# Fourier mixing and an ELU layer on one core: VectorE's combinations and transposes at other places of the order, one small transfer on GpSimd's queue

## The chip, the cores and the metric

The kernel runs on one core of a Trainium2 chip. The core has TensorE (matrix products; the profile calls its matmuls PE and its weight loads PEld), VectorE (DVE), ScalarE (ACT), GpSimd (POOL) and a queue engine, SyncE (SP), which here only issues transfers. The metric is the device time of one execution in microseconds (us): the median over eight runs. Lower is better.

## The reference

```python
def _attn_ref(x):                       # x: (8, 3008, 256) float32
    X = np.fft.fft(x, axis=1)
    X = np.fft.fft(X, axis=2)
    return X.real.astype(np.float32)

def _moe_ref(x, w_in, w_out):           # x: (24064, 256)
    h = x @ w_in                        # w_in (256, 2048)
    g = np.where(h > 0.0, h, np.exp(np.minimum(h, 0.0)) - 1.0)
    return (g @ w_out).astype(np.float32)   # w_out (2048, 256)
```

The result of the first goes, as 24064 rows of 256, into the second. The two weight matrices arrive as 64-bit floats.

## The kernel before

**Work.** The transform along the sequence is done as products with cosine and sine matrices (`Dft`); the one along the channels is folded into `w_in`, which becomes a cosine part `Wc` and a sine part `Ws`. Symmetry lets one column serve two output rows: h is P plus Q for one row and P minus Q for its mirror, with P from `Wc` and Q from `Ws`. Transformed columns are kept in three rings, `Rr` (real part), `Ir` (imaginary part, the "sine ring") and `Rb` (channel 128 on all partitions). Channel 128 has no row in the 128-row product; its weights are the last row of `Ws`, which is carried to columns of `wex` through a scratch row in memory, `wx` (`spread_last_row`, line 389: two transfers per chunk of 256 columns, the second of which waits for the first).

**Steps and tiles.** A tile is 256 columns; there are 47. Each takes eight steps, each for 256 of the 2048 hidden units, so 376 steps in all. A step is spread over three periods of the order: `mm_P` (TensorE, bank `H`), `even_part` (two VectorE instructions that add channel 128's part, `E <- Rb, wex, H`, line 714), `mm_Q` (adds Q to the same bank, and therefore must follow `even_part`), `h_minus` (VectorE, line 724), exponentials on ScalarE, `g_plus` and `g_minus` (VectorE, line 740), four sums on GpSimd (`sum_1`, `sum_3`, `sum_2`, `sum_4`, line 362), and the second product with `w_out`. This one is done in Winograd's way, with seven products instead of eight: `mm_X1` writes banks `pA` and `pB`, `mm_X2` writes `pC` and `pD`, and they gather over the eight steps of a tile. At a tile's end VectorE combines the banks: `comb_1` makes `u` from `pA` (through a copy by ScalarE) and `pB`; `comb_2` makes `v` from `u` and `pC`; `comb_22` adds `v` and `pC` into half of `u`; `comb_3` adds `pD` to `v`. Then `turn_u` and `turn_v` transpose `u` and `v`, and SP stores them. The first tile has the plain eight products, and the first eight steps also run beside the preparation of the weights.

**Order.** Everything runs in an order written out by hand: `at(t, fn)` puts a function at time t, in units of about one microsecond, and the list is sorted and emitted once. A period `T` is 4.8 units. Each engine works through its own instructions in this order, so t decides only who stands before whom on an engine. Within a step's first period VectorE has `even_part` at 0.9, then of the step before `g_plus` at 2.2 and `g_minus` at 2.9, then `h_minus` at 3.55. TensorE has `mm_P` at 0, `mm_X1` of two steps before at 0.87, `mm_Q` at 2.17, `mm_X2` at 3.04, and at 4.75 in some steps half of a `Dft`, whose results VectorE puts into the rings at 1.01 and 1.02 of the next period (`plus`, `minus`).

**Weights.** A weight chunk passes through `fields` (VectorE), `power` (ScalarE), `round` and `scale` (VectorE or GpSimd) (lines 203 to 270). Folded input sums are made by `fold_x`; `EO1` and `EO3` are the sums that the odd frequencies need.

Of the kernel before, what the change touches and what calls it, by code (L numbers as in the profile page):

```python
# [77 lines left out]
def kernel(  # L78
# [7 lines left out]
    nc = tc.nc  # L86
# [78 lines left out]
    Ws = cpool.tile([128, NDFF], FP, tag="Ws")  # L165
# [177 lines left out]
    wx_dr = dpool.tile([1, NDFF], FP, tag="wx", name="wx")  # L343
# [44 lines left out]

    def spread_last_row(q):
        c = slice(q * 256, (q + 1) * 256)  # L390
        nc.sync.dma_start(out=wx_dr[:, c], in_=Ws[127:128, c])
        with nc.allow_non_contiguous_dma(reason="one row to columns"):
            nc.sync.dma_start(
                out=wex[:, 2 * q : 2 * q + 2],
                in_=wx_dr[:, c].rearrange("o (f p) -> p (o f)", p=128),
            )
# [608 lines left out]
    def fold_now(keys):  # L1005
        for key in keys.split():
            ops[key, 0]()
# [9 lines left out]
    def at(t, fn):  # L1017
        events.append((t, len(events), fn))

    def at_chunk(t, chunk):  # L1020
        at(t, chunk.fields)
        at(t + 0.01, chunk.power)
        at(t + 0.02, chunk.round)
        at(t + 1.4, chunk.scale)
# [31 lines left out]
        dft_now(state["x_even"], 0, "pD")  # L1056

    at(-12.8, begin_x_even)
    at(-12.6, lambda: spread_last_row(0))
    at(-11.0, lambda: fold_now("O2 o0 o1 O0 EO2"))  # L1060
    at_chunk(-10.0, w1_chunks[1])
    at(-8.5, R_even.copy)
# [6 lines left out]
    at(-5.8, lambda: state["x_even"].minus())  # L1069
    at(-5.7, lambda: nc.sync.dma_start(out=Ir[127:128, 0:RUN], in_=Rb[127:128, 0:RUN]))  # L1070
    at_chunk(-5.0, w1_chunks[2])
    at(-1.9, lambda: fold_now("EO1 EO3"))
    at(-1.7, w1_chunks[6].load)
    at(-1.6, w1_chunks[7].load)
    at(-1.5, w2_chunks[3].load)
# [3 lines left out]
    T = PERIOD  # L1079
    for chunk, k, second in (  # L1080
        (w1_chunks[3], 0, 0),
        (w2_chunks[0], 0, 1),
        (w1_chunks[4], 1, 0),
        (w2_chunks[1], 1, 1),
        (w1_chunks[5], 2, 0),
        (w2_chunks[2], 2, 1),
        (w1_chunks[6], 3, 0),
        (w2_chunks[3], 3, 1),
        (w1_chunks[7], 4, 0),
        (w2_chunks[4], 4, 1),  # L1090
        (w2_chunks[5], 5, 1),
        (w2_chunks[6], 6, 1),
        (w2_chunks[7], 7, 1),
    ):
        t = k * T + (1.0 if second else -0.5)
        at(t, chunk.fields)
        at(t + 0.02, chunk.power)
        at(t + 0.05, chunk.round)
        at(k * T + (3.7 if second else 1.7), chunk.scale)
    for c in range(1, 8):  # L1100
        t = (c - 2) * T + 4.7 if c > 1 else 1.0
        at(t, lambda c=c: fold_chunk(c))
        t = (c - 1) * T + 1.4 if c > 1 else 2.0
        at(t, lambda c=c: put_chunk(c))
        at(t + 0.01, lambda c=c: spread_last_row(c))
# [13 lines left out]
    for i in range(total):  # L1119
        t = i * T  # L1120
# [20 lines left out]
    COMB = (  # L1141
        (1.45, comb_copy),
        (4.2, comb_1),
        (T + 1.0, comb_2),
        (T + 1.1, comb_22),
        (T + 1.2, comb_3),
    )
    for q in range(n_tiles):
        t = (8 * q + 9) * T
        for dt, fn in (COMB if q else ((1.45, plain_u), (T + 1.1, plain_v))) + (  # L1150
            (2 * T + 1.0, turn_u),
            (3 * T + 1.0, turn_v),
        ):
            at(t + dt, lambda fn=fn, q=q: fn(q))

# [55 lines left out]
    for n in range(16):  # L1211
        j, k = divmod(n, 4)
# [87 lines left out]
```

## Time and profile before

| | |
|---|---|
| median of 8 runs | 2009.41 us (2008.33 to 2011.47) |
| profiled execution | 2007.74 us, of it 2006.0 us span |
| TensorE matmuls busy | 1975.1 us, 98% of the span |
| VectorE busy | 1277.3 us, 64% |
| ScalarE busy | 860.8 us, 43% |
| GpSimd busy | 1330.3 us, 66% |
| share of the chain that ended last | TensorE 92%, transfers 3%, VectorE 2%, GpSimd 1%, ScalarE 1% |
| transfers | 71.6 MB, mean 36 GB/s; the 16 transfer engines are near full in the first 36 us |

The span runs from the first to the last instruction of one profiled execution. Busy times overlap. An engine's idle time is put down to what ended it. Matmul records overlap too, so a busy TensorE can still lose time between two matmuls: the distance from one start to the next has to be read. A 128x256 product in this kernel is two matmul instructions, and their starts stand 0.216 us apart when nothing holds them.

### The profile page before, as it was taken

How to read it: one execution, taken by the hardware profiler on the slowest of the kernel's cores; microseconds unless marked ns; L12 is line 12 of the kernel's file. 1: busy time of each engine (PE TensorE's matmuls, PEld its weight loads, DVE VectorE, ACT ScalarE, POOL GpSimd, SP SyncE). 2: the span in 40 equal slices, each digit the busy share in tenths (PEclk: the TensorE clock that was granted, in tenths of full speed). 3: DMA queues.
4: the chain of work that ended last, by engine and by line, in shares of the span. 5: the costliest groups of instructions: out<-in, count | busy, mean ns of one | idle time of the engine just before them, and what ended most of it. 6: DMA issues, size and time to landing. Idle time of an engine off the chain costs nothing.

```text
span 2006.0 us, 26767 instructions
## 1 busy us (share of the span) xinstructions
PE 1975.1 (98%) x8895; PEld 1655.3 (83%) x8896; DVE 1277.3 (64%) x2342; ACT 860.8 (43%) x1651; POOL 1330.3 (66%) x1818
## 2 busy tenths in 40 slices
PE   8899999999999999999999999999999999999997
PEld 4788888888888888888888888888888888888886
DVE  7866656666566656666566665666556665666665
ACT  2544444443444444444444443444434444444443
POOL 2577757776577766777567775678657776555564
PEclk9999999999999999999999999999999999999999
DMA  8227200121001110011100211003010110000101
GB/s 318 85 20 64 48 16 13 38 60 22 13 19 43 45 29 11 18 47 43 26 18 13 65 24 26 11 19 90 7 19 11 23 18 15 15 11 16 18 11 21
DMA packets 256253, 71.60 MB, mean 36 GB/s; under 512 B 244512, under 2 KB 245302, under 8 KB 255604
## 3 DMA queue, kind: packets, MB, share of 16 engines
q1 hardware_dynamic: 253780, 57.32, 14.5%
q0 software_dynamic: 2336, 12.59, 1.9%
q8 instruction: 70, 1.15, 0.2%
q14 instruction: 67, 0.55, 0.1%
HBM read 45.02 MB, written 24.80 MB: 35 GB/s over the span
## 4 chain that ended last, share of the span: by engine, by line
PE 92%; DMA 3%; DVE 2%; POOL 1%; ACT 1%; issue 1%; DVEq 0%; SPq 0%; POOLq 0%; ACTq 0%
PE H L353 37%; PE pB L353 16%; PE pC L353 16%; PE pD L353 15%; PE pA L353 8%; DMA wx<-Ws 1%; POOL G L362 1%; DVE E L714 1%; DMA xl<-in_x_dram,ix 1%; DMA wex<-wx 0%; DMA w<-in_moe_w_out_dram 0%; DVE G L740 0%; DMA xl<-in_x_dram 0%; POOL xl L144 0%; ACT w L365 0%
## 5 line engine op out<-in xcount | busy, mean ns | idle before, releaser
L362 POOL TENSOR_TENSOR G<-G 128x256 f32<-128x256 f32 x1472 | 1055.4, 728 | 599.9 <-DVE G L740 438.0
L714 DVE SCALAR_TENSOR_TENSOR E<-Rb,wex,H 128x256 f32<-128x256 f32 x752 | 328.0, 478 | 647.2 <-PE H L353 642.7
L365 ACT ACTIVATE G<-H 128x512 f32<-128x512 f32 x376 | 224.5, 597 | 969.4 <-DVE G L724 969.4
L353 PE MATMUL H<-Ir,Ws 128*128 128x256 f32 x1504 | 387.7, 380 | 13.7 <-DVE E L714 13.7
L353 PE MATMUL H<-Rr,Wc 128*128 128x256 f32 x1504 | 386.4, 379 | 0.0
L353 PE MATMUL pC<-G,WT 128*128 128x256 f32 x1472 | 381.1, 381 | 2.3 <-DVE u L359 2.3
L353 PEld LDWEIGHTS H<-Ir,Ws 128*128 128x128 f32 x1504 | 278.8, 190 | 62.2 <-DVE E L714 16.8
L353 PEld LDWEIGHTS H<-Rr,Wc 128*128 128x128 f32 x1504 | 285.1, 190 | 53.2 <-issue 2.5
L353 PEld LDWEIGHTS pC<-G,WT 128*128 128x128 f32 x1472 | 276.0, 190 | 52.8 <-issue 13.6
L740 DVE SCALAR_TENSOR_TENSOR G<-G,H 128x512 f32<-128x512 f32 x376 | 253.4, 674 | 33.4 <-ACT G L365 32.2
L724 DVE SCALAR_TENSOR_TENSOR G<-E,H 128x512 f32<-128x512 f32 x376 | 256.0, 681 | 25.4 <-PE H L353 0.9
L740 DVE SCALAR_TENSOR_TENSOR G<-M,G 128x512 f32<-128x512 f32 x376 | 256.4, 682 | 0.0
L353 PE MATMUL pA<-G,w 128*128 128x256 f32 x800 | 234.2, 379 | 0.5 <-issue 0.5
L353 PE MATMUL pB<-G,w 128*128 128x256 f32 x800 | 234.0, 379 | 0.0
L365 ACT ACTIVATE G<-G 128x512 f32<-128x512 f32 x376 | 233.3, 620 | 0.0
L353 PE MATMUL pB<-G,WT 128*128 128x256 f32 x736 | 224.3, 386 | 1.4 <-POOL G L362 1.3
L365 ACT ACTIVATE M<-G 128x512 f32<-128x512 f32 x376 | 224.3, 596 | 0.0
L365 ACT ACTIVATE M<-M 128x512 f32<-128x512 f32 x376 | 221.0, 588 | 0.1
L353 PE MATMUL pD<-G,w 128*128 128x256 f32 x736 | 218.9, 379 | 0.0
L353 PE MATMUL pD<-G,WT 128*128 128x256 f32 x736 | 218.9, 379 | 0.0
L353 PEld LDWEIGHTS pA<-G,w 128*128 128x128 f32 x800 | 151.8, 190 | 21.9 <-POOL w L362 0.9
L353 PEld LDWEIGHTS pB<-G,w 128*128 128x128 f32 x800 | 152.0, 190 | 20.7
(134 smaller groups left out, 1329.2 us busy)
## 6 DMA issues: line engine op xcount, KB each, us to landing
out_dram<-ot SPq DMA_DIRECT2D x504, 32.0 KB
xl<-in_x_dram SPq DMA_DIRECT2D x16, 768.0 KB
MC<-dft_mats SPq DMA_DIRECT2D x4, 1131.0 KB
out_dram<-ot SPq DMA_DIRECT2D x256, 2.0 KB
Rb<-r SPq DMA_DIRECT2D x10, 376.0 KB
raw<-in_moe_w_in_dram SPq DMA_DIRECT2D x6, 512.0 KB
raw<-in_moe_w_out_dram SPq DMA_DIRECT2D x6, 512.0 KB
out_dram<-ot SPq DMA_DIRECT2D x64, 28.0 KB
```

Source lines behind the costliest of these rows:

```text
L353: nc.tensor.matmul(out_, lhsT=lhsT, rhs=rhs, start=start, stop=stop, skip_group_check=True)
L362: pin(nc.gpsimd.tensor_tensor(out=o, in0=a, in1=b, op=op))
L365: pin(nc.scalar.activation(out=o, in_=i, func=func, **kw))
L714: nc.vector.scalar_tensor_tensor(out=S.E[:, c], in0=Rb[:, cols(i)], scalar=wex[:, f : f + 1], in1=S.H[:, c], op0=ALU.mult, op1=ALU.add,)
L724: nc.vector.scalar_tensor_tensor(out=two(S.G[:, 0:512])[:, :, ::-1], in0=two(S.E), scalar=2.0, in1=two(S.H), op0=ALU.mult, op1=ALU.subtract,)
L740: nc.vector.scalar_tensor_tensor(out=o, in0=e, scalar=-1.0, in1=h, op0=ALU.add, op1=ALU.max)
```

## The change

Five things move; no arithmetic is added or taken away.

1. The first chunk's last row (`spread_last_row(0)`) is issued by GpSimd's queue instead of SP's, and earlier in the order (from -12.6 to -13.05, just behind `put_chunk(0)`, which writes that row).
2. The odd sums `EO1`, `EO3` go from -1.9 to 0.5, behind the first write of the sine ring (`I_even.plus`, `minus`, at 0.0 and 0.1).
3. `fields`, `power` and `round` of the weight chunk of step 0 (`w1_chunks[3]`) go from -0.5 to 0.3, also behind those writes.
4. At a tile's end `comb_2` and `comb_22` go from behind the next step's `even_part` to ahead of it, directly behind `comb_1`; `comb_3` goes from ahead of `g_plus` to behind it.
5. `turn_u` and `turn_v` go from behind `even_part` to behind `h_minus` of the same period.

```diff
     def spread_last_row(q):
         c = slice(q * 256, (q + 1) * 256)
-        nc.sync.dma_start(out=wx_dr[:, c], in_=Ws[127:128, c])
+        queue = nc.sync if q else nc.gpsimd
+        queue.dma_start(out=wx_dr[:, c], in_=Ws[127:128, c])
         with nc.allow_non_contiguous_dma(reason="one row to columns"):
-            nc.sync.dma_start(
+            queue.dma_start(
                 out=wex[:, 2 * q : 2 * q + 2],
...
-    at(-12.6, lambda: spread_last_row(0))
+    at(-13.05, lambda: spread_last_row(0))
...
-    at(-1.9, lambda: fold_now("EO1 EO3"))
+    at(0.5, lambda: fold_now("EO1 EO3"))
...
-        t = k * T + (1.0 if second else -0.5)
+        t = k * T + (1.0 if second else 0.3 if k == 0 else -0.5)
...
     COMB = (
         (1.45, comb_copy),
         (4.2, comb_1),
-        (T + 1.0, comb_2),
-        (T + 1.1, comb_22),
-        (T + 1.2, comb_3),
+        (4.21, comb_2),
+        (4.22, comb_22),
+        (T + 2.5, comb_3),
     )
...
-            (2 * T + 1.0, turn_u),
-            (3 * T + 1.0, turn_v),
+            (2 * T + 4.2, turn_u),
+            (3 * T + 4.2, turn_v),
```

## The prediction

> **What bounds the kernel.** I read the page's shares first (matmuls busy 98% of the span, TensorE 92% of the chain), so time can come only from places where TensorE loses starts. The view of waits names them (who waited for what: us in total, times, longest):
>
> ```profile
> DVE E L714 <- PE H L353: 642.7, 367, 3.9
> ...
> PEld pB L353 <- POOL G L362: 17.6, 52, 1.0
> ...
> PE H L353 <- DVE E L714: 13.7, 7, 7.0
> ...
> PEld pC L353 <- issue: 13.6, 42, 0.3
> ...
> DVE E L714 <- DMA wex<-wx: 4.5, 3, 2.9
> ```
>
> VectorE waits for `mm_P` nearly every step, 1.75 us each: the gap ahead of `even_part` that the change wants to fill. TensorE waits at three places: once 7.0 us at the start, 42 times for `pC`, 52 times for `pB`. I then read the timeline of VectorE and TensorE at one tile's end (start, length, what; idle before it in brackets):
>
> ```profile
> 361.91 0.68 DVE L724 SCALAR_TENSOR_TENSOR G<-E,H 128x512 f32<-128x512 f32 x1
> ...
> 362.50 0.68 DVE L359 TENSOR_TENSOR u<-p,pB 128x512 f32<-128x512 f32 x1
> ...
> 364.09 0.87 DVE L714 SCALAR_TENSOR_TENSOR E<-Rb,wex,H 128x256 f32<-128x256 f32 x2 [0.91 <-PE H L353]
> ...
> 364.88 0.68 DVE L359 TENSOR_TENSOR v<-u,pC 128x512 f32<-128x512 f32 x1
> 365.01 0.79 PEld L353 LDWEIGHTS H<-Ir,Ws 128*128 128x128 f32 x4
> 365.18 1.03 PE L353 MATMUL H<-Ir,Ws 128*128 128x256 f32 x4
> 365.59 0.42 DVE L359 TENSOR_TENSOR u<-v,pC 128x256 f32<-128x256 f32 x1
> 366.05 0.69 DVE L359 TENSOR_TENSOR v<-v,pD 128x512 f32<-128x512 f32 x1
> 366.13 0.73 PEld L353 LDWEIGHTS pC<-G,WT 128*128 128x128 f32 x4 [0.32 <-issue]
> 366.16 1.10 PE L353 MATMUL pC<-G,WT 128*128 128x256 f32 x4
> ...
> 369.75 0.30 PEld L353 LDWEIGHTS pB<-G,WT 128*128 128x128 f32 x2 [0.30 <-POOL G L362]
> ```
>
> Four matmuls take 0.86 us from start to start, but 0.98 from `mm_Q` (365.18) to `pC` (366.16), and 0.94 on to `pD`: 0.19 lost. The profile says "issue"; the row that ends just before, at 366.01, is `comb_22`, the last reader of `pC`. A step later the weight load for `pB` waits for GpSimd's `sum_2`, late because `g_plus` and `g_minus` stood behind three combinations: 0.17 lost. A weight load that starts x late costs x - 0.12 (0.31 late cost 0.19; 0.28 late cost 0.17).
>
> **Combinations, what goes.** The timelines of all 45 ends at which another step follows show the `pC` loss: 45 x 0.19 = 8.6 us; in three of them (near 980, 1027, 1432 us) ring writes stand between `comb_2` and `comb_22` and it is some 0.85 more each: 2.5. The `pB` loss follows 37 ends: 37 x 0.17 = 6.1. Together 17.2.
>
> **What is added: the combinations ahead of `even_part`.** `mm_Q`'s weight load in ordinary steps starts 0.05-0.06 after `even_part` ends, so it has only 0.07 to spare. From `comb_1`'s start to `even_part` there are 1.59 us (362.50 to 364.09). `comb_2` depends on `comb_1`, `comb_22` on `comb_2`: 0.71 each, as 364.88 to 365.59 shows. `comb_22` to `even_part` is independent; independent rows stand 0.08 closer than their length (0.68 long, 0.59 or 0.60 apart), so 0.34. Sum 1.76: `even_part` 0.17 to 0.18 late, TensorE loses 0.11. The distance is 1.56 to 1.59 at 28 ends: 3.1 us. At 9 ends VectorE is already late from ring writes and the distance is 1.10 to 1.25 (mean 1.20): 0.56 late, 0.49 lost, 4.4 us. At 8 ends half a `Dft` stands ahead of `mm_P` and it is 3.5 to 3.8: nothing. Sum 7.5. The bounds of this unseen adjacency: nothing if the load could go on the first half of `even_part`; 0.12 more per end (37 x 0.12 = 4.4) if `comb_22` is followed as by `comb_3`, 0.46 later. I take 0.34, the spacing of independent rows.
>
> `pC` is ready: its last matmul of the tile ends near 362.3. **`comb_3`** behind `g_plus` starts at 362.50 + 1.76 + 0.79 + 0.60 = 365.65 and ends at 366.34; `pD`'s load is due at 366.8. Behind it `g_minus` ends at 366.93 instead of 367.93; two sums of 0.75 after it end near 368.5, and `pB` needs them at 369.5, so that loss goes. At the three ends with ring writes `comb_3` ends near 980.96 where the load is due at 980.5: 0.45 each, 1.4 in all. Net of the combinations: 17.2 - 7.5 - 1.4 = 8.3 us.
>
> **Transposes**: 94 x 0.70 us, hidden in the gap of 1.85 us (1.2 after ring writes). If that cover were gone each would cost up to 0.6. Beside GpSimd's work one already takes 0.70 (374.73, under an L425 row). Their 1272 stores leave SP some 2.4 us later; SP issues 16 in 9.5 us, twice per 38 us. Last tile: same sequence. Nothing.
>
> **The start.**
>
> ```profile
> 23.39 0.30 SPq L391 DMA_DIRECT2D wx<-Ws  x1
> ...
> 30.53 1.57 POOL L362 TENSOR_TENSOR w<-raw,w 128x512 f32<-128x512 f32 x1 [26.21 <-ACT w L365]
> 30.87 2.04 DVE L425 TENSOR_TENSOR o<-o,o 128x762 f32<-128x762 f32 x1
> ...
> 38.51 0.87 DVE L714 SCALAR_TENSOR_TENSOR E<-Rb,wex,H 128x256 f32<-128x256 f32 x2 [2.94 <-DMA wex<-wx]
> ...
> 39.44 2.08 PE L353 MATMUL H<-Ir,Ws 128*128 128x256 f32 x4 [7.04 <-DVE E L714]
> ```
>
> The row is written at 18.8, goes out at 23.39 and lands at 35.45 (12.06 us in the chain); the second transfer takes 2.9 more. Only then runs the first `even_part`, and TensorE stands 7.04 us. Here a rule speaks against the change. The row: SP's queue holds whole matrices ahead of these 1 KB, and earlier GpSimd's two loads of x, 1.5 MB, landed in 10.55 us beside 3.3 MB of SP's. The Trainium skill (DMA: Bandwidth & Descriptors, "Issuing engines are not separate DMA queues") says that transfers from all engines share the same 16 engines and that a second issuer saves little but issue time. By it `wex` still lands near 38 and nothing is gained; by the row a second queue gets its turns between the first one's packets. I take the row. Issue 19.1, two transfers: the low end is GpSimd's shortest landing, 1.9 us each (near 23); the high end is 16 packets of 4 bytes per engine in turn with packets of 0.35 us (the longest kind in the transfer records here), 16 x 0.36 + 2 for the second and 4 for the first (near 31). Either is before 35.5, GpSimd's own next work is at 30.53, and SP's loads behind the removed pair go out 6 us sooner, for steps 15 us away or more.
>
> Then VectorE's own order binds. Ring writes wait for ScalarE's copy (30.83): 30.87 to 31.86. Chunk fields 0.75, `EO1`/`EO3` 1.9. The 2.04 row (its like takes 0.95) and GpSimd's 1.57 (1.29 alone) show that such pairs hold each other up; one GpSimd product of 1.1 falls between. Sum: 31.86 + 0.75 + 1.1 + 1.9 = 35.6, against 38.51: 2.9 us. TensorE's chain from there to 48.46 is back to back and later waits hang on it, so the shift stays.
>
> The clock (busy us per engine, then granted clock, transfer share, GB/s):
>
> ```profile
> 32.00:36.00 4.00, 0.39 (x2) 0.00 (x0) 3.56 (x5) 1.65 (x3) 1.96 (x2) 0.96 0.99 403
> 36.00:40.00 4.00, 0.56 (x1) 0.50 (x2) 1.49 (x5) 0.39 (x2) 1.29 (x1) 0.50 0.76 259
> 40.00:44.00 4.00, 4.00 (x11) 2.63 (x10) 3.10 (x6) 2.68 (x6) 2.37 (x2) 0.69 0.65 227
> ```
>
> After the idle stretch the clock is half until 42.5, so 3.05 us of work cost 1.5 more. The Trainium skill (TensorE: Matmul & The Clock Gate, "What's actually happening") has one idle window of 3.4 us, free-running, lower the clock. By the trace's row alone any idle of this kind costs 1.5; by the rule the 4.1 us that remain (32.4 to 36.5) hold a whole window only in (4.1 - 3.4) / 3.4 = a fifth of phases. I take the rule: 1.5 gained; if the clock still falls, -1.5 to +1.5. The start: 4.4 us.
>
> **Sum.** 8.3 + 4.4 = 12.7 us. The profiled execution, 2007.7 us (span 2006.0), would become 1995.0; its time is 1.7 below the median, so the median goes from 2009.4 to **1996.7**.
>
> **Rivals.**
> - `wex` through GpSimd lands no sooner than 38.5, or the half clock eats it: the start gives nothing, 2001.1. For: the shared engines, full until 38 us. Against: GpSimd's loads above. With the dearer 0.46 spacing too, 2005.5. Chance 0.23.
> - `even_part`'s lateness is free: 1996.7 - 7.5 = 1989.2. For: it has two halves. Against: the load stands 0.05 behind the second one's end in every ordinary step. Chance 0.09.
> - Slower: `comb_2` is released only when the next `mm_P` is through, so `even_part` is 1.05 late at 37 ends: 37 x 0.98 - 7.5 = 28.8 more, 2025.5. It decides from about 0.66 us lost per end. Against: in the last tile `comb_2` starts at 1993.48, 0.03 after `pC`'s matmul ends. Chance 0.08.
> - The forecast: 0.60, own range 1993 to 2000.
>
> What a measurement tells from no change is about 0.2%, 4 us: 2005.4 to 2013.4. The first rival reaches into that band with its dear end (0.10 in all). Range 1989 to 2005.5.
>
> **What would show it.** `PEld pC <- issue` and most of the 52 `pB` waits gone; a new `PEld H <- DVE E` wait of about 0.2 at some 28 ends and 0.55 at 9; `even_part` first at 35.6; granted clock 1 from 36 to 42. If the `H` waits exceed 0.6 on average, or the first `E` still waits for `wex`, the forecast is wrong there.

## The result, and the profile after

The changed kernel takes 1998.92 us (median of 11 runs, 1997.54 to 2006.24) against 2010.1 us (32 runs). By these medians it is 11.2 us less; the forecast was 12.7 us less, 1996.7 us. The ratio that is given here and below weighs all runs and is not that of the medians; three of the 11 runs lie above 2005 us. It is 0.9952, 95% interval 0.9943 to 0.9961: 9.6 us less, between 7.8 and 11.5. The profiled execution took 1999.07 us, 1997.3 of it span.

The waits of the whole changed kernel (who waited for what: us in total, times, longest):

```profile
PEld H L353 <- DVE E L715: 29.2, 44, 5.2
...
PE H L353 <- DVE E L715: 9.0, 14, 2.4
...
PE H L353 <- DMA Ir<-Rb: 4.8, 1, 4.8
...
DVE E L715 <- DMA wex<-wx: 1.9, 2, 1.4
...
PEld pB L353 <- POOL G L362: 1.7, 3, 0.9
PEld pD L353 <- PE pC L353: 1.7, 3, 0.6
```

The 42 waits at `pC` are gone and of 52 at `pB` 3 are left. In their place 44 weight loads of `mm_Q` wait for `even_part`, and three of `pD` wait at ends with ring writes. In the kernel before, the first of these lines read:

```profile
PEld H L353 <- DVE E L714: 16.8, 8, 7.4
```

At the start a transfer that no wait of before named, `Ir<-Rb`, now ends TensorE's longest wait, of 4.8 us. It brings the row of channel 128 from `Rb` into the sine ring, which `mm_Q` reads. The two waits for `wex` that are left belong to later chunks; the first `even_part` no longer waits for it.

The timeline of the changed kernel at the tile's end that the prediction read:

```profile
361.87 0.68 DVE L359 TENSOR_TENSOR u<-p,pB 128x512 f32<-128x512 f32 x1
...
362.65 0.69 DVE L359 TENSOR_TENSOR v<-u,pC 128x512 f32<-128x512 f32 x1
...
363.37 0.42 DVE L359 TENSOR_TENSOR u<-v,pC 128x256 f32<-128x256 f32 x1
...
363.71 0.86 DVE L715 SCALAR_TENSOR_TENSOR E<-Rb,wex,H 128x256 f32<-128x256 f32 x2
...
364.50 0.68 DVE L741 SCALAR_TENSOR_TENSOR G<-G,H 128x512 f32<-128x512 f32 x1
364.63 0.73 PEld L353 LDWEIGHTS H<-Ir,Ws 128*128 128x128 f32 x4 [0.32 <-DVE E L715]
364.63 1.13 PE L353 MATMUL H<-Ir,Ws 128*128 128x256 f32 x4
365.09 0.68 DVE L359 TENSOR_TENSOR v<-v,pD 128x512 f32<-128x512 f32 x1
```

The chain is 0.78 + 0.72 + 0.34 = 1.84 us long, where the prediction had 0.71 + 0.71 + 0.34 = 1.76. `even_part` no longer waits for anything: it is late. It ends at 364.57, the weight load of `mm_Q` starts 0.06 us later, and TensorE's starts lose 0.19 us here.

To part the start from the rest I use `comb_1`, which runs once per tile from the second on. The view of tile `u`, first of the kernel before, then of the changed one (count, shortest/median/longest in ns, first and last start in us):

```profile
L359 DVE TENSOR_TENSOR u<-p,pB x46: 677/679/686, 152.5 to 1992.7; 128x512 f32<-128x512 f32 x46
```

```profile
L359 DVE TENSOR_TENSOR u<-p,pB x46: 677/679/687, 152.7 to 1983.9; 128x512 f32<-128x512 f32 x46
```

From the first to the last it is 1840.2 us before and 1831.2 after, 9.0 less. The first comes no sooner, 152.7 against 152.5. In this execution the tiles' ends bring all and the start nothing.

The start of the changed kernel, in its timeline:

```profile
28.41 0.62 SPq L1071 DMA_DIRECT2D Ir<-Rb  x1
...
36.49 0.86 DVE L715 SCALAR_TENSOR_TENSOR E<-Rb,wex,H 128x256 f32<-128x256 f32 x2
...
37.52 2.04 PE L353 MATMUL H<-Ir,Ws 128*128 128x256 f32 x4 [4.81 <-DMA Ir<-Rb]
...
39.36 3.95 PE L353 MATMUL pA<-MC,e 128*128 128x376 f32 x6
```

`even_part` is 2.0 us sooner (38.51 before), `mm_Q` 1.9 (39.44). `even_part` ended at 37.35, so the transfer itself held `mm_Q` for little more than 0.1 us; both come at nearly the same time. But the six matmuls of `pA` now take 3.95 us (2.65 before). The windows of the changed kernel show why (busy us of PE, PEld, DVE, ACT, POOL, then granted clock, transfer share, GB/s):

```profile
32.00:36.00 4.00, 0.72 (x4) 0.29 (x2) 4.00 (x4) 1.92 (x3) 2.70 (x2) 1.00 0.99 402
36.00:40.00 4.00, 2.48 (x6) 1.86 (x7) 3.01 (x7) 2.28 (x5) 0.40 (x1) 0.54 1.04 386
40.00:44.00 4.00, 4.00 (x9) 2.27 (x8) 3.96 (x5) 2.32 (x5) 3.99 (x3) 0.61 0.61 196
```

The clock is half from 36.3 to 43.2 us. Work now falls into 5.6 us of that, not 3.05, and loses 2.8 us, not 1.5. So of 1.9 us, 0.6 are left at the second step's `even_part` (47.83 against 48.48). The changed kernel has one more stretch of half clock, 77.3 to 80.7 us, which this profile of the kernel before has not. The fifth step's `mm_Q`, just before it is through, still comes 0.5 us sooner (77.42 against 77.96); the sixth's comes at the same time (86.03 against 86.01) and waits for nothing but TensorE's own work. So the rest was lost in between, where that stretch lies.

### The profile page after: what moved, and what is told of

It reads as the page before. It is cut to its first block, busy times and chain, and to the rows that moved or that the text cites. A ratio compares the mean times of both kernels' runs of the same rounds, so it can differ in the third digit from the quotient of the medians.

```text
span 1997.3 us, 26765 instructions
## 1 busy us (share of the span) xinstructions
PE 1968.9 (99%) x8895; PEld 1662.0 (83%) x8896; DVE 1284.7 (64%) x2342; ACT 861.3 (43%) x1651; POOL 1336.5 (67%) x1820
## 3 DMA queue, kind: packets, MB, share of 16 engines
q8 instruction: 70, 1.15, 0.2%
## 4 chain that ended last, share of the span: by engine, by line
PE 93%; DVE 4%; ACT 1%; DMA 1%; issue 1%; POOL 0%; DVEq 0%; ACTq 0%; POOLq 0%; SPq 0%
PE H L353 38%; PE pB L353 16%; PE pD L353 16%; PE pC L353 15%; PE pA L353 8%; DVE E L715 1%; PE M L353 1%; DVE G L741 1%; DVE u L359 0%; DMA Ir<-Rb 0%; DVE v L359 0%; DVE G L725 0%; ACT G L365 0%; DMA wx<-Ws 0%; DVE w L220 0%
## 5 line engine op out<-in xcount | busy, mean ns | idle before, releaser
L353 PE MATMUL H<-Ir,Ws 128*128 128x256 f32 x1504 | 392.4, 383 | 13.8 <-DVE E L715 9.0
L353 PE MATMUL pB<-G,WT 128*128 128x256 f32 x736 | 219.2, 379 | 0.5 <-POOL G L362 0.5
L353 PEld LDWEIGHTS pB<-G,w 128*128 128x128 f32 x800 | 152.7, 191 | 21.0
```

The costliest lines, as they stand in the source:

```text
L353: nc.tensor.matmul(out_, lhsT=lhsT, rhs=rhs, start=start, stop=stop, skip_group_check=True)
```

## The experiments

Theory A, formed from the two traces: the gain is all at the tiles' ends, and at the start the sine ring's row and the half clock leave nothing of it. Theory B, the recorded forecast: the start carries 3 to 4 us. All ratios are to the kernel before, run on the same chip.

**Tiles' ends alone, start alone.** `steady_only` is the kernel before with the `COMB` and `turn` lines of the change's diff, `start_only` with the others.

> Parts 4 and 5 of the change alone (combinations, transposes), the start as before. Theory A (all of the gain is at the tiles' ends; the start's two us are lost again to the sine ring's row and the half clock): 8 to 9.5 us faster than before, the same time as the changed kernel within 1.5 us. Theory B (the start carries some 3 to 4 us of it): 5 to 6 us faster than before, 3 to 4 us slower than the changed kernel. In the trace under both: TensorE loses no start at pC, some 0.19 us at 27 ends and 0.56 at 9 ahead of mm_Q.

> Parts 1 to 3 alone (row on GpSimd's queue, odd sums and chunk fields behind the sine ring), tiles' ends as before. Theory A: 0 to 1.5 us faster than before; first even_part near 36.5 us, mm_Q near 37.5, waiting for the transfer Ir<-Rb. Theory B: 3 to 4 us faster.

Measured: `steady_only` 0.9959 (0.9947 to 0.9972), 8.2 us faster; `start_only` 0.9997 (0.9988 to 1.0005), not told from no change. The view of tile `u` of `steady_only` and of `start_only`:

```profile
L359 DVE TENSOR_TENSOR u<-p,pB x46: 678/681/689, 152.9 to 1985.7; 128x512 f32<-128x512 f32 x46
```

```profile
L359 DVE TENSOR_TENSOR u<-p,pB x46: 680/681/689, 153.0 to 1993.5; 128x512 f32<-128x512 f32 x46
```

1832.8 us between first and last, as in the changed kernel within 1.6, and 1840.5, as before. Of the 1.6, 1.2 are one wait for channel 128 in this execution of `steady_only`. Theory A holds and theory B is refuted: by the 95% interval of `start_only` the start is worth 2.4 us at most. Whether it is worth anything stays open; the medians differ by 1.5 us (2008.67 against 2010.15). In `start_only` the first `even_part` ran at 36.62 us, and `mm_Q` at 37.94, 0.4 behind its end. The profile puts this wait down to a VectorE instruction that `mm_Q` does not read (`pow`, line 214), not to `Ir<-Rb` as was expected.

**comb_22 behind even_part.**

```diff
         (4.21, comb_2),
-        (4.22, comb_22),
+        (T + 1.0, comb_22),
         (T + 2.5, comb_3),
```

> The changed kernel with comb_22 alone put back behind even_part (T + 1.0); comb_2 stays ahead of it. Theory A (TensorE loses what even_part comes late by: chain 0.78 + 0.72 + 0.34 = 1.84 us against 1.58 there): the chain becomes 0.78 + 0.60 = 1.4 us, so the 27 losses of 0.19 go and the 9 of 0.56 become some 0.15; pC's load is due 0.5 us after comb_22's end, so no wait returns: 8 to 10 us faster than the changed kernel, near 1989.5. Rival: comb_22 was not what made it late, or pC's wait comes back: within 2 us of the changed kernel.

Measured: 0.9911 (0.9898 to 0.9923), median 1991.1 us; 0.0041 below the changed kernel's ratio, 8.2 us. Its timeline at the same end:

```profile
360.04 0.68 DVE L359 TENSOR_TENSOR u<-p,pB 128x512 f32<-128x512 f32 x1
...
360.82 0.69 DVE L359 TENSOR_TENSOR v<-u,pC 128x512 f32<-128x512 f32 x1
...
361.62 0.87 DVE L715 SCALAR_TENSOR_TENSOR E<-Rb,wex,H 128x256 f32<-128x256 f32 x2
...
362.41 0.41 DVE L359 TENSOR_TENSOR u<-v,pC 128x256 f32<-128x256 f32 x1
362.55 0.79 PEld L353 LDWEIGHTS H<-Ir,Ws 128*128 128x128 f32 x4
...
363.36 0.62 PEld L353 LDWEIGHTS pC<-G,WT 128*128 128x128 f32 x3
```

`even_part` starts 1.58 us behind `comb_1`, as it did in the kernel before; `mm_Q`'s load has no wait, and `comb_22` ends at 362.82, half a microsecond before `pC`'s load. Its waits:

```profile
PEld H L353 <- DVE E L715: 17.3, 17, 4.9
...
PEld pD L353 <- PE pC L353: 2.7, 3, 0.9
```

17 loads wait for `even_part`, not 44. By the starts of TensorE's matmuls the losses ahead of `mm_Q` fell from 10.5 us to about 1. Those at `pD`, at the three ends with ring writes, grew from 1.3 to 2.3, where `comb_22` now runs between `even_part` and `comb_3`. That `even_part`'s lateness is the change's main price is thereby shown, and all but 1 us of it could have been avoided. From the first to the last `comb_1` it takes 1822.9 us, 8.3 less than in the changed kernel.

**TensorE kept busy at the start.**

```diff
+    def keep_busy():
+        t = bank("pB")
+        for _ in range(18):
+            mm(t, zero, zero[:, 0:1].to_broadcast([128, 512]), True)
+
+    at(2.1, keep_busy)
```

> The changed kernel with 18 matmuls of zeros added ahead of the first mm_Q, in TensorE's idle stretch (their result is not used). Theory A (the clock falls to half after the idle stretch and stays there to about 43 us, costing up to 2.8 us): granted clock 1 from 32 to 44 us, pA's first six matmuls 1.9 us instead of 3.7, 1 to 3 us faster than the changed kernel and less spread. Rival (the half clock costs nothing since the later steps wait for VectorE, ScalarE and transfers anyway): same time within 1 us though the clock is whole.

Measured: 0.9944 (0.9932 to 0.9957), median 1997.01 us; the interval overlaps the changed kernel's, so by time alone it is not told from it. The trace tells more; its windows and its view of `u`:

```profile
32.00:36.00 4.00, 4.00 (x20) 2.02 (x19) 4.00 (x5) 1.92 (x3) 2.84 (x3) 1.00 0.99 404
36.00:40.00 4.00, 3.12 (x13) 1.90 (x11) 4.00 (x9) 2.10 (x5) 0.21 (x1) 1.00 1.03 384
40.00:44.00 4.00, 4.00 (x16) 2.81 (x16) 3.13 (x4) 2.32 (x5) 4.00 (x3) 1.00 0.64 220
```

```profile
L359 DVE TENSOR_TENSOR u<-p,pB x46: 680/681/687, 150.2 to 1981.5; 128x512 f32<-128x512 f32 x46
```

`mm_Q` starts no sooner (37.59) and the clock stays whole. The second step's `mm_Q`, first in the changed kernel, then here:

```profile
48.76 1.13 PE L353 MATMUL H<-Ir,Ws 128*128 128x256 f32 x4 [0.97 <-DVE E L715]
```

```profile
46.06 1.13 PE L353 MATMUL H<-Ir,Ws 128*128 128x256 f32 x4 [0.96 <-DVE E L715]
```

From the first `mm_Q` to the second it is 8.5 us, not 11.2: the 2.8 that half of 5.6 us says. The first `comb_1` comes 2.5 us sooner than in the changed kernel. In the nine profiled executions without these matmuls (the kernel before among them) it came between 151.7 and 154.4 us. So the trace shows the gain, but the times do not, and the spread of the runs, which was expected to shrink, did not (1996.36 to 2004.52).

**Combinations alone, transposes alone.** The two parts of `steady_only`.

> The kernel before with the combinations moved as in the change (part 4) and nothing else; the transposes stay behind even_part. Theory A (the waits at pC and pB both come from the three combinations; the transposes are hidden at either place): as fast as steady_only within 1.5 us, 8 to 9 us faster than before, hardly any wait of pB at the tiles' ends. Rival (the transposes are what makes g_minus and the sum for pB late): the waits of pB stay, 2 to 3 us faster than before only.

> The kernel before with the transposes alone moved (part 5). Theory A: within 1 us of before; waits at pC and pB as before. Rival: some 6 us faster, since the waits of pB go.

Measured: `comb_only` 0.9976 (0.9965 to 0.9987), 4.8 us faster, so 3.4 us short of `steady_only`: a miss. `turn_only` 0.9997 (0.9986 to 1.0007), medians 2007.48 against 2009.99. Theory A said that the transposes don't matter; the waits of `turn_only` say that they do a little (52 times and 17.6 us before):

```profile
PEld pB L353 <- POOL G L362: 14.4, 43, 0.7
```

In `comb_only` 12 waits of `pB` stay, 4.7 us, against 3 and 1.7 us in `steady_only`. The two differ in the place of the transposes alone: ahead of `g_plus` they make some of GpSimd's sums late. By the starts of TensorE's matmuls this costs 1.8 us of the 3.4. Another part may be what is seen in `comb_only`'s profiled execution, the slowest of its runs, in its waits from 185 to 206 us:

```profile
POOL xs L362 <- DMA xs<-xe_dr: 7.0, 1, 7.0
...
PE H L353 <- POOL xe L362: 6.1, 1, 6.1
```

Channel 128's rows of the other batches come as single 4-byte values through SP; here they landed after TensorE stood at their product. That execution took 2011.86 us, the median is 2004.88.

**The row alone.** Part 1 of the change: the odd sums and chunk fields keep their old place.

> The kernel before with part 1 alone: the row on GpSimd's queue; odd sums and chunk fields stay ahead of the sine ring's writes. Theory A (once wex is early, two things end together: VectorE's work ahead of the first even_part, and the transfer of the sine ring's row on SP's queue near 37.4 us): first even_part near 35.6 us, since the order with the sums first loses less to GpSimd's products, but mm_Q still near 37.4, waiting for Ir<-Rb; time as start_only within 1 us, 0 to 1.5 us faster than before. Rival (the new order of the sums is what brings the start its two us): even_part no sooner than 38, time as before.

Measured: 0.9992 (0.9983 to 1.0002). Its timeline:

```profile
35.89 0.86 DVE L715 SCALAR_TENSOR_TENSOR E<-Rb,wex,H 128x256 f32<-128x256 f32 x2
...
37.61 1.80 PE L353 MATMUL H<-Ir,Ws 128*128 128x256 f32 x4 [4.14 <-DMA Ir<-Rb]
```

As theory A said: without parts 2 and 3 the first `even_part` is 0.6 us sooner than in the changed kernel, and `mm_Q` is where it was, held by the sine ring's row 0.9 us beyond the end of `even_part` (36.75). Parts 2 and 3 brought the start nothing.

**A combined version, twice.** `best` and `best2` put `comb_22` and `comb_3` directly behind `even_part`, and keep the transposes in the gap, part 1, and the filler (the 18 matmuls of zeros); `best` also moves the sine ring's row to GpSimd's queue, `best2` leaves that row on SP and puts channel 128's chain one period later. `ext_late` is the changed kernel with that last edit alone.

```diff
+        (4.21, comb_2),
+        (T + 1.0, comb_22),
+        (T + 1.005, comb_3),
```

```diff
-    at(25 * T + 1.35, fold_ext)
-    at(25 * T + 4.75, dft_ext)
+    at(26 * T + 1.35, fold_ext)
+    at(26 * T + 4.75, dft_ext)
```

(and `ext_side`, `ext_rows` likewise)

> What the runs so far point to: comb_2 ahead of even_part, comb_22 and comb_3 directly behind it, transposes in the gap, sums and fields of the start in the old order, the first chunk's row and the sine ring's row both on GpSimd's queue, and 18 matmuls of zeros in TensorE's idle stretch ahead of the first mm_Q (their result is not used). Theory A: first mm_Q near 36.5 us, clock whole; no wait of 0.7 at pD at the three ends with ring writes; 4 to 6 us faster than comb22_behind, near 1986. Rival: the two rows on GpSimd's queue are no sooner than on SP's, and the start is as in keep_busy: near 1988 to 1989.

`best` missed: 0.9906 (0.9893 to 0.9919), median 1993.23 us. Its runs lie far apart: 1987.32 and 1987.86, near what was expected, then 1993.23, 1995.19 and 1998.64. The profiled execution is the last of these. Its waits from 180 to 210 us:

```profile
POOL xs L362 <- DMA xs<-xe_dr: 5.8, 1, 5.8
...
PE H L353 <- POOL xe L362: 5.1, 1, 5.1
```

Channel 128 again, and half clock from 195.3 to 202.1 us, beginning within that wait. Its start was late before any part of the change: the loads of x let VectorE begin on them at 12.45 us instead of 10.26 (before), and from the last write of `Rb` to the first `even_part` it took 7.76 us, just as in `row_only` (28.13 to 35.89). On TensorE it looked so (one of the 18 records is missing):

```profile
35.91 4.08 PE L353 MATMUL pB<-zero 128*128 128x512 bf16 x17
...
39.83 1.02 PE L353 MATMUL H<-Ir,Ws 128*128 128x256 f32 x4
```

The sine ring's row landed 4.9 us after its issue at 31.09 on GpSimd's queue, where it took 9.0 on SP's in the changed kernel (28.41 to 37.39), and `even_part` ended at 38.87. So neither held `mm_Q`: the filler did, which with this late start ran some 0.9 us too long. The row is early on GpSimd's queue, but what that is worth this execution can't tell.

> The changed kernel with the chain of channel 128 (fold_ext, dft_ext, ext_side, ext_rows) one period later, so that TensorE comes to it some 5 us later against its transfers. Theory A (the executions of the changed kernel near 2005 to 2006 us are those in which the 4-byte transfers of channel 128 land after TensorE stands at dft_ext, as the profile of comb_only shows with 6.2 us): none above 2002 us any more, the rest as in the changed kernel, 1997 to 1999.5. Rival (they have another cause): 2005 to 2006 us appear as before, in about one of four.

> comb_2 ahead of even_part, comb_22 and comb_3 directly behind it, transposes in the gap, the first chunk's row on GpSimd's queue, sums and fields of the start in the old order, the sine ring's row on SP as before, 18 matmuls of zeros ahead of the first mm_Q (their result is not used), and the chain of channel 128 one period later. Theory A: no loss of 0.7 at pD, clock whole at the start, no late channel 128: median 1986 to 1988, spread under 4 us. Rival (the start's gain is lost at later waits, or comb_3 directly behind even_part brings pB's wait back): 1990 to 1993.

`ext_late`: 0.9946 (0.9932 to 0.996), five runs from 1998.68 to 2000.37 us. None was near 2005, as theory A said; but three of the changed kernel's 11 were there, and five runs would miss such ones one time in five anyway, so this fits and doesn't settle it. `best2`: 0.9897 (0.9881 to 0.9912), median 1989.31 us, 1989.07 to 1991.11: faster than both kernels, 20.7 us below before, a little short of what was expected. From `comb22_behind` alone (0.9911) the intervals don't tell it. Its start:

```profile
32.91 4.08 PE L353 MATMUL pB<-zero 128*128 128x512 bf16 x18
37.60 1.10 PE L353 MATMUL H<-Ir,Ws 128*128 128x256 f32 x4 [0.61 <-DMA Ir<-Rb]
```

The sine ring's row still sets `mm_Q` there. The clock is whole at the start and half from 74.6 to 78.0 us; the first `comb_1` comes at 150.3 us, as in `keep_busy`. From there to the last it takes 1825.6 us, 2.7 more than `comb22_behind`. At the three ends with ring writes the wait at `pD` is gone, but `pB` waits 0.6 us instead, since `g_plus` now stands behind `comb_3`. And channel 128 is late in this execution too, the slowest of the four, though its chain comes a period later:

```profile
PE H L353 <- POOL xe L362: 1.3, 1, 1.3
```

`comb22_behind` with the filler added, which these numbers favour, was not run.

## Why the prediction came out as it did

- **Combinations, what goes** (17.2 us). Right and too small. Added up from the starts of TensorE's matmuls, the `pC` loss of 11.0 us went whole, as worked out; the `pB` loss fell from 10.6 to 1.3 us, 9.3 where 6.1 was said. Counted were only the waits one step behind a tile's end; others hung on the transposes, which alone take 2.0 off the `pB` loss in `turn_only` (8.6 left).
- **What is added ahead of `even_part`** (7.5 us). Right in kind, place and count, mis-sized: 0.19 us at 28 ends and 0.57 at 9, 10.5 us together. The term at fault is `comb_1` to `comb_2`, set at 0.71 after the row of `comb_2` to `comb_22`; it measured 0.78. The last tile had shown 0.79 and was put down to `pC`.
- **`comb_3` and `pD`** (1.4 us): 1.3 measured at the same three ends. **Transposes at nothing**: they gain some 2 us, by `turn_only`'s trace (153.7 to 1991.6 us from first to last `comb_1`, 2.3 less than before), too little for its times to tell.
- **Net of the tiles' ends** (8.3 us). `steady_only` 8.2, the trace of the changed kernel 9.0; by the starts 11.0 + 9.3 - 10.5 - 1.3 = 8.5. Two errors of 3 us each, one for and one against, cancel: the mechanism was right, that the net came out so near is luck.
- **The row on GpSimd's queue.** The reading of the row was right, against the rule that the prediction cites beside it: `wx` landed 4.8 us after its issue instead of 12.1, so a second queue saved much more than issue time while SP's held whole matrices.
- **"Then VectorE's own order binds", 35.6 us, 2.9 us gained.** This failed twice. `even_part` came at 36.49, since two rows and not one ran into GpSimd's products (`w<-raw` took 1.50 instead of 0.42, `o<-o,o` 2.05). And VectorE was not alone: `mm_Q` also reads the sine ring, whose last row left SP at 28.41 behind the same matrices and landed near 37.4. I had asked what was next late on VectorE and not what else `mm_Q` waits for. With the forecast `even_part` at 35.6 the row would have cost nearly 1 us, as it did in `row_only`; behind 36.49 it cost 0.1. That "the shift stays" failed as well: by the sixth step it was gone.
- **The clock, 1.5 us gained.** Failed. The idle stretch was still 4.8 us (32.7 to 37.5), and in all five profiled executions with an earlier start and no filler (the changed kernel, `start_only`, `row_only`, `comb22_behind`, `ext_late`) the clock fell to half near 35 to 38 us. With the earlier restart, more work fell into the half-rate stretch. Taking "a fifth of phases" from the rule was too hopeful: in `ext_late` the window ahead of the fall held 0.58 us of TensorE's work in 3.41.
- **The rivals.** That the start gives nothing was one, at 2001.1 us with a chance of 0.23; its mechanism (`wex` no sooner) was wrong, its half clock right. The measured 1998.9 lies between it and the forecast. A free lateness is refuted by the 0.19 us that TensorE's starts lose and by the 8 us of `comb22_behind`, a release behind `mm_P` by `comb_2`, which starts 0.78 behind `comb_1`.
- **The sum** (12.7 us). 11.2 by the medians, 9.6 by the ratio. The ends gave what was said; the 4.4 of the start are the term that failed, with nothing in the trace and 2.4 at most by `start_only`.

What stays open is how often, and why, channel 128's transfers land late. Four profiles show the wait: 6.1 us in `comb_only` and 5.1 in `best`, each with a stretch of half clock, 1.2 in `steady_only` and 1.3 in `best2`. So a period more did not always suffice. That it makes up the changed kernel's three runs above 2005 us is not shown, and no run varied the transfers themselves.

## What to carry to other kernels

When work is put into an engine's idle gap, what counts is not how long the engine is idle but when it can start the next instruction that another engine needs. Add up the dependent chain that is put ahead of it (here 1.84 us into 1.59), and move out the one link that is not needed yet (here `comb_22`, worth 8 us). Before a wait is counted as gained, list every input of the instruction that waited, and where each stands in its queue. At the start of a kernel, a stretch of half clock can eat an earlier restart. Filling the idle engine kept the clock and 2.5 us in the trace, but a filler of fixed length can itself hold up the work behind it, as in `best`.

## What the runs showed of the hardware

- In the first 210 us of these traces every stretch of half clock lasted 3.4 or 6.8 us, so I looked at TensorE's work in the 3.41 us ahead of one. The half clock did not need a wholly idle window: windows with 0.58 us (`ext_late`, 31.95 to 35.36 us) and 1.15 us (changed kernel, 73.9 to 77.3 us) of matmul time were followed by half clock. One with 1.66 us (`comb22_behind`, 74.4 to 77.9 us) was not.
- A 1 KB row on GpSimd's queue took 4.8 us (changed kernel, issued at 19.4) where the same row took 12.1 on SP's (before, issued at 23.4), both with the transfer engines' share near 1. The sine ring's row took 4.9 (`best`) against 9.0 (changed kernel).
